# Batches 0 and 1 of an attention on 64x32 tiles, all engines in one written order until unit 32

## The chip, the core and the metric

The kernel runs on one core of one Trainium2 chip. The core has a matrix engine (TensorE, PE in the rows; PEld is its weight load), a vector engine (VectorE, DVE), a scalar engine (ScalarE, ACT), a general engine (GpSimd, POOL) and a queue engine that issues the DMAs (SyncE, SP). The metric is the device time of one launch in microseconds. Three runs of the kernel before took 1621.26 to 1624.84 us, with a median of 1621.86 us.

## The reference

Three layers follow one another: a two-step attention, a feed-forward layer with a leaky rectifier, and a gated feed-forward layer.

```python
# q, k, v: 8 batches, 8 heads, 576 tokens, 64; p: 8, 8, 32, 64
p_packed = sm_attn(p, k, v)                  # softmax(scale * p k^T) v
x = sm_attn(q, p_packed, p_packed)           # to 4608 tokens x 512
h = x @ w_in                                 # 512 x 2048
g = np.maximum(h, 0.0) + alpha * np.minimum(h, 0.0)
x = g @ w_out                                # 2048 x 512
g = x @ w_gate                               # 512 x 1536
out = (g / (1.0 + np.exp(-g)) * (x @ w_val)) @ w_out2
```

## The kernel before

The first feed-forward layer is cut into 256 units: 16 token halves of 288 tokens (batch b, half), times 16 blocks f of 128 hidden columns. A unit has an h part (`h_unit`, six 128x288 matmuls on `a2`, the attention weights, and `ppw`, the product of packed values and `w_in`), then ScalarE, VectorE, ScalarE and GpSimd make the rectified `g32` and its split in a rounded `hi` and a rest `lo`. Three units later its o part (`o_unit`, twelve 128x288 matmuls) adds to four PSUM banks `acc0` to `acc3`. A run of units with one token half ends with the four banks being emptied; where the sum is not complete, it goes to DRAM as `x1p` and is read again by `load_part` and added at the end of that token half's next run. Units are numbered in the order of the list `order`.

`w_in` and `w_out` come as 16 pieces of 1 MB in a 64-bit format (`i0` to `i14`, `o0` to `o14`, two blocks f each) and are widened to 32 bits: two ScalarE, three VectorE (lines 244, 248, 257) and two GpSimd instructions a piece; a `w_out` piece is then rounded (`round_piece`). `ppw` of batch b and four blocks f (`pp_win`, the words `w00`, `w01` and so on) needs two `w_in` pieces and the batch's packed values.

Batches 2 to 7 have their attention in `attention(b)`: its small matmuls work on 64x32 tiles of the PE array, eight heads at a time (`heads8`), its k and q are loaded in 128-byte pieces and turned by VectorE, and its steps are laid between units by the table STEPS. Batches 0 and 1 have theirs in `quad(g)`, four heads at a time on 128x64 tiles, with k and q turned by PE; four quads a to d. Their steps, the loads and the pieces are ordered by LOADS, START, EARLY and ORDER; a scheduler sets the order on each engine within these. The first 64 units are of batches 0 and 1, in runs of eight blocks f; units 64 to 255 are of batches 2 to 7, in runs of sixteen.

While units go on, from slot GROUP0 (half a unit is a slot) the weights of the last layer are widened too (`more_weights2`). The last layer starts after unit 255.

Of the kernel before, what the change touches and what calls it, by code (L numbers as in the profile page):

```python
# [81 lines left out]
GROUP0 = 84  # L82
# [20 lines left out]
def f32(ap):  # L103
    return ap.bitcast(F32)


@with_exitstack
def tile_kernel(
# [105 lines left out]
    raws, vals, borrowed, queue, marks, spots = [], [], [], [], {}, {}  # L214
    fetched, loaded, unsplit = [], [], []
# [9 lines left out]
    def load():  # L225

        src, parts, f = queue.pop(0)
        raw = raws.pop(0)
        fetch(like(raw, src), src)
        loaded.append((raw, parts, f))  # L230

    def fetch(out, in_):

        with tc.issue_after(fetched[-1].ins) if fetched else ExitStack():
            fetched.append(nc.sync.dma_start(out=out, in_=in_))

    def widen(raw, val):
# [3 lines left out]
        nc.scalar.activation(out=f32(val), in_=f32(high), func=AF.Abs)  # L241
        nc.scalar.activation(out=low, in_=low, func=AF.Copy, scale=2.0**-29)
# [22 lines left out]
        yield "v"  # L265
        yield "v"
# [4 lines left out]
    def convert():  # L271

        raw, parts, f = loaded.pop(0)
        dst = parts()
        spots["piece"] = spots.get("piece", -1) + 1
        if f is None:
            val = dst[0].bitcast(U32)
        else:
            val = vals.pop(0) if len(vals) > 1 else vals[0]
        for _ in widen(raw, val):  # L280
            pass
        if queue and (spots["piece"] < 4 or not any(raw is t for t in borrowed)):
            raws.append(raw)
            load()
        unsplit.append((dst, val, f))

    def round_piece():

        dst, val, f = unsplit.pop(0)
        for i in range(2 if f is not None else 0):  # L290
# [6 lines left out]
            nc.gpsimd.tensor_tensor(out=lo, in0=full, in1=f32(hi), op=ALU.subtract)  # L297

# [14 lines left out]
    make_identity(nc, ident)  # L313
    ppbd = [sm.tile([P, P], F32, name=f"ppbd{i}") for i in range(2)]
    for t in ppbd:
        nc.vector.memset(t, 0.0)
    al = sm.tile([P, NF1], F32, name="al")
    sg = sm.tile([P, NF1], F32, name="sg")
    sal = sm.tile([P, NF1], F32, name="sal")
    spare = sm.tile([P, 1], F32, name="spare")  # L320
    a2, ppT = {}, {}

    def quad(g, ptags=("at",), evac=nc.scalar):

# [37 lines left out]
        def s_v():  # L362
            st["v"] = load_n(v, "v")
# [1281 lines left out]
```

## Time and profile before

| | us |
|---|---|
| median of three runs | 1621.86 |
| the profiled execution | 1619.38 |
| its span, first to last instruction | 1617.6 |
| PE busy in the span | 1557.8 |
| VectorE, ScalarE, GpSimd busy | 999.8, 777.7, 986.5 |

The profile is of one execution. Busy time is time in which an engine ran an instruction of the program; "idle before" names what ended an engine's wait. PEclk is the TensorE clock that was granted, as a share of full speed; its mean over the span is 0.989. A tile name such as `h` stands for all buffers of that name.

### The profile page before, as it was taken

To read this page: it belongs to the slowest core of one execution; us is meant where nothing else is said; L and a number is where in the kernel's file an instruction comes from. 1 tells how busy PE (TensorE), PEld (TensorE's weight loads), DVE (VectorE), ACT (ScalarE), POOL (GpSimd) and SP (SyncE) were. 2 spreads that over 40 slices of the span, in tenths; PEclk is the share of its full clock that TensorE was granted. 3 is DMA by queue.
4 is the path that set the end of the run, shared out by engine and by line. 5 is a ranking of instruction groups with operands and counts; after the bars stand their busy time and mean duration, and the time that the engine had idled before them with its cause. 6 is when DMAs were issued, how large, how long until landed. Compare 5 with 4: busy or idle time off the path is not lost.

```text
span 1617.6 us, 30288 instructions
## 1 busy us (share of the span) xinstructions
PE 1557.8 (96%) x10967; PEld 1467.5 (91%) x10967; DVE 999.8 (62%) x1788; ACT 777.7 (48%) x1722; POOL 986.5 (61%) x1057
## 2 busy tenths in 40 slices
PE   6589999999999999999999999999999999999997
PEld 3368898989898989889999999999999999999997
DVE  5856557564646556474346765685686676578556
ACT  6577655666565656565443333333333333333322
POOL 3637655767676665657266566665666656666653
PEclk8799999999999999999999999999999999999999
DMA  9515365756555564653567788688688777866962
GB/s 293 146 43 149 103 167 152 187 146 174 139 166 158 143 178 129 176 172 112 192 228 270 258 280 279 239 295 273 250 301 247 276 277 264 292 240 245 295 251 70
DMA packets 296358, 333.88 MB, mean 206 GB/s; under 512 B 193536, under 2 KB 247824, under 8 KB 291600
## 3 DMA queue, kind: packets, MB, share of 16 engines
q1 hardware_dynamic: 296208, 331.94, 64.2%
q8 instruction: 86, 1.41, 0.4%
q14 instruction: 64, 0.52, 0.1%
HBM read 276.05 MB, written 55.84 MB: 205 GB/s over the span
## 4 chain that ended last, share of the span: by engine, by line
PE 83%; DVE 6%; ACT 4%; issue 2%; DMA 2%; POOL 1%; SPq 1%; ACTq 0%; POOLq 0%; DVEq 0%
PE acc L1099 7%; PE acc L1105 7%; PE acc L1100 7%; PE yb L308 5%; PE yb L310 4%; PE yb L309 4%; PE h L308 4%; PE h L310 3%; PE h L309 3%; PE xb L308 3%; PE vb L309 3%; PE vb L308 3%; PE vb L310 3%; PE xb L309 3%; PE xb L310 3%
## 5 line engine op out<-in xcount | busy, mean ns | idle before, releaser
L1086 POOL TENSOR_TENSOR lo<-g,hi 128x288 fp32r<-128x288 f32 x256 | 219.5, 861 | 208.9 <-ACT hi L1084 150.0
L1076 DVE SCALAR_TENSOR_TENSOR g<-h,sg,m 128x288 f32<-128x288 f32 x256 | 130.7, 512 | 214.9 <-ACT m L1073 179.2
L1309 POOL TENSOR_TENSOR s<-s,u 128x384 f32<-128x384 f32 x72 | 73.0, 1014 | 210.1 <-ACT s L1302 210.1
L1341 POOL TENSOR_TENSOR s<-s,s 128x384 f32<-128x384 f32 x141 | 150.2, 1065 | 48.0 <-DVE s L1306 34.2
L1263 DVE TENSOR_TENSOR u<-yb,p 128x384 f32<-128x384 f32 x144 | 80.0, 556 | 157.5 <-PE yb L310 132.8
L308 PE MATMUL h<-a2h,ppw 128*128 128x288 f32 x512 | 158.9, 310 | 14.2 <-ACT a2h L543 7.1
L1073 ACT ACTIVATE m<-h,sal 128x288 f32<-128x288 f32 x256 | 127.1, 497 | 87.5 <-PE h L310 87.0
L1084 ACT ACTIVATE hi<-g 128x288 fp32r<-128x288 f32 x256 | 112.7, 441 | 93.0 <-DVE g L1076 85.9
L309 PE MATMUL h<-a2h,ppw 128*128 128x288 f32 x512 | 151.8, 297 | 0.0
L310 PE MATMUL h<-a2l,ppw 128*128 128x288 f32 x512 | 151.5, 297 | 0.0
L1335 POOL TENSOR_TENSOR fl_S<-s,fh_S 128x384 fp32r<-128x384 f32 x142 | 147.1, 1045 | 0.2
L308 PE MATMUL yb<-ring,gv 128*128 128x384 f32 x432 | 145.5, 337 | 1.4 <-DVE u L1263 1.4
L310 PE MATMUL yb<-ring,gv 128*128 128x384 f32 x432 | 144.4, 334 | 0.0
L309 PE MATMUL yb<-ring,gv 128*128 128x384 f32 x432 | 144.4, 334 | 0.0
L308 PEld LDWEIGHTS h<-a2h,ppw 128*128 128x128 f32 x512 | 97.1, 190 | 44.0 <-issue 16.2
L1263 DVE TENSOR_TENSOR u<-vb,u 128x384 f32<-128x384 f32 x144 | 80.0, 556 | 81.3 <-PE vb L310 80.9
L1335 POOL TENSOR_TENSOR fl_A<-s,fh_A 128x384 fp32r<-128x384 f32 x108 | 113.3, 1049 | 25.2 <-ACT fh_A L1331 23.9
L1302 ACT ACTIVATE s<-p 128x384 f32<-128x384 f32 x72 | 37.8, 525 | 179.5 <-DVE p L1263 179.5
L1331 ACT ACTIVATE fh_S<-s 128x384 fp32r<-128x384 f32 x144 | 72.7, 518 | 70.2 <-POOL s L1341 67.4
L966 POOL TENSOR_TENSOR cva<-cva,cva 128x256 fp32r<-128x256 f32 x126 | 92.6, 744 | 12.7 <-ACT cva L965 12.2
L308 PE MATMUL xb<-ring,gv 128*128 128x384 f32 x288 | 98.5, 342 | 1.6 <-ACT p L1285 1.4
L309 PEld LDWEIGHTS h<-a2h,ppw 128*128 128x128 f32 x512 | 97.5, 190 | 0.0
(298 smaller groups left out, 4923.9 us busy)
## 6 DMA issues: line engine op xcount, KB each, us to landing
gv<-wgvd SPq DMA_DIRECT2D x144, 896.0 KB, 7.4
wp<-wo2d SPq DMA_DIRECT2D x36, 1024.0 KB, 5.1
wp<-wo2d SPq DMA_DIRECT2D x36, 768.0 KB, 4.5
wgvd<-cva SPq DMA_DIRECT2D x84, 256.0 KB, 2.8
wo2d<-cva SPq DMA_DIRECT2D x42, 256.0 KB, 2.8
v<-in_v_dram SPq DMA_DIRECT2D x16, 576.0 KB, 5.2
cva<-in_moe_w_in_dram SPq DMA_DIRECT2D x7, 1024.0 KB, 7.6
kr<-in_k_dram SPq DMA_DIRECT2D x96, 72.0 KB, 2.8
```

Of the source, the lines that this page charges most:

```text
L308: nc.tensor.matmul(o, wlo, xhi, start=start, stop=False, **kw)
L309: nc.tensor.matmul(o, whi, xhi, start=False, stop=False, **kw)
L310: return nc.tensor.matmul(o, whi, xlo, start=False, stop=stop, **kw)
L1073: begun[it] = marks[f"u{it}"] = nc.scalar.activation(out=m, in_=hp, func=AF.Copy, scale=sal[:, f : f + 1])
L1076: made[it] = marks[f"m{it}"] = nc.vector.scalar_tensor_tensor(out=g32, in0=hp, scalar=sg[:, f : f + 1], in1=m, op0=ALU.mult, op1=ALU.max)
L1086: nc.gpsimd.tensor_tensor(out=lo, in0=x, in1=f32(hi), op=ALU.subtract)
L1099: nc.tensor.matmul(acc[dc], lo[:, f % WP, c], ghi, start=start, stop=False)
L1100: last = nc.tensor.matmul(acc[dc], hi[:, f % WP, c], ghi, start=False, stop=False)
L1105: last = nc.tensor.matmul(acc[dc], hi[:, f % WP, c], glo, start=False, stop=stop)
L1263: ins = nc.vector.tensor_tensor(out=out, in0=bank, in1=x, op=ALU.add)
L1335: return (nc.vector if by_dve else nc.gpsimd).tensor_tensor(out=lo, in0=x, in1=f32(hi), op=ALU.subtract)
L1341: engine.tensor_tensor(out=out, in0=x, in1=y, op=op)
```

## The change

`quad` goes away. All eight batches use `attention(b)`, so the matmuls of batches 0 and 1 work on 64x32 tiles too, with eight heads at once. Batch 0 is special: its k is still turned by PE (`s_turn_pe`), its q comes in groups of four heads (`s_half`), its heads are dealt to the tiles by `head0`, its packed values are kept twice, and its second softmax is done by halves of 288 tokens. Batch 1 loads k and q in 128-byte pieces, as batches 2 to 7 do.

START is now one list of all steps up to unit 31, units included: h and O words are the parts of a unit (each word advances it by one engine's share), C and R widen and round a piece, l loads one, w makes a `ppw` (a and b are its column halves), D stores and X loads a partial sum. `Lane` ties every instruction of these steps to the one before it on its engine, so the engines keep that order. The rest of the pieces (`i12`, `i14`, `o12`, `o14`) is laid into units 32 to 51 by LATER, and GROUP0 goes from 84 to 104.

The order of units is now: batch 0's two halves with blocks 0 to 3, the same with blocks 4 to 7, batch 1's halves with blocks 0 to 7, then all four halves with blocks 8 to 11, and all four with blocks 12 to 15. Until unit 63 there are 14 runs in place of 8.

The rectifier is written differently (`rests`, `h_unit`): ScalarE makes max(-h, 0), and VectorE multiplies that by 1 - alpha and adds h. The signs that were folded into `w_out` go, and with them one ScalarE instruction for each half of a `w_out` piece. `widen` yields "v" three times a piece in place of five, which `more_weights2` counts.

```diff
-LOADS = "a.k pd b.k l al a.v b.v l a.q b.q l l"
+LOAD_PART = 4
...
 START = """
-    a.kt0 b.kt0 a.pt a.kt1 b.kt1 b.pt 1 turn a.s1 a.et a.pp b.s1 1:E0,mx1 sign:mx1 c.k c.q c.v a.ppt b.et
...
+    0.v1 0.k0 lo0 al 0.k1 0.p 0.kt0 0.v0 0.kt0 0.k2 Co0 turn 0.k3 li2 turn 0.kt1 Co0 sign 0.pt 0.kt1
+    0.pt 0.q0 Co0 Co0 0.kt2 Co0 0.kt2 0.kt3 Co0 0.kt3 0.q1 0.s11 Ro0 0.s10 Ci2 Ro0 0.mx0 Ci2 1.p 0.mx1
...
+SCRIPTED = 32
+RAWS = """
+    i0:0 i2:1 o0:2 o2:3 i4:4 i6:0 o4:1 o6:2 i8:0 i10:1 o8:0 o10:1 i12:0 i14:1 o12:0 o14:0
+"""
...
-GROUP0 = 84
+GROUP0 = 104
...
+class Lane:
...
+        def call(*args, **kwargs):
+            if not self.held:
+                return fn(*args, **kwargs)
+            with self.tc.issue_after(self.last.ins) if self.last else ExitStack():
+                self.last = fn(*args, **kwargs)
+            return self.last
...
-        yield "v"
-        yield "v"
         yield "p"
...
             full = like(f32(val), dst[0])[:, i, :]
-            nc.scalar.activation(
-                out=full, in_=full, func=AF.Copy, scale=sg[:, f + i : f + i + 1]
-            )
             nc.scalar.activation(out=hi, in_=full, func=AF.Copy)
...
         with behind():
             for i in range(H // 2):
                 for r in range(2):
-                    rows, n = slice(64 * r, 64 * r + 64), slice(32 * i, 32 * i + 32)
+                    n = slice(32 * i, 32 * i + 32)
                     last = nc.tensor.matmul(
-                        out[r][n], lhs[rows, n], rhs[i][rows], start=True, stop=True
+                        out[r][n], lhs(r, n), rhs(r, i), start=True, stop=True
...
+    def head0(r, i):
+
+        return 4 * r + (i ^ r)
+
+    def lhs_of(b, r, e, n):
+
+        if b == 0:
+            n = slice(P * r + n.start, P * r + n.stop)
+        return ppT[b][rows(e), n]
...
+        def s_half(half):
+
+            t = wide[half][:, : 2 * S]
+            for i in range(2):
+                st["q"][2 * half + i] = t[:, i * S : (i + 1) * S]
+            for r in range(2):
+                h = 4 * r + 2 * half
+                src = q[b, h : h + 2].rearrange("i (t j) (e x) -> e j (i t) x", j=32, x=32)
+                for e in range(2):
+                    blk = 2 * r + e
+                    nc.sync.dma_start(
+                        out=t[32 * blk : 32 * blk + 32].rearrange("p (t x) -> p t x", x=32),
+                        in_=src[e],
+                    )
...
+        def s_turn_pe(i):
...
+                for x in range(M6 // 2):
+                    nc.tensor.transpose(
+                        tp[:, x * PB : (x + 1) * PB],
+                        st["k"][i][:, hh, x * P : (x + 1) * P],
+                        ident[:PB, :PB],
+                    )
...
+            for half in range(2) if first else (None,):
+                c = 14 + 2 * r + half if first else 4 + r
+                nc.scalar.activation(
+                    out=e[:, span(half)],
+                    in_=st["s1"][half][r] if first else e,
+                    func=AF.Exp,
+                    bias=sums[:, 2 + r : 3 + r],
+                    scale=SCALE,
+                    accum_out=sums[:, c : c + 1],
+                )
...
+        def s_rest(r, half=None):
+            hi, lo = (t[:, span(half)] for t in a2[b, r])
+            engine = nc.gpsimd if early else nc.vector
+            engine.tensor_tensor(
+                out=lo, in0=st["a"][r][:, span(half)], in1=f32(hi), op=ALU.subtract
+            )
...
+    def pp_win(b, j, c=slice(0, 512)):
+
+        if (b, j) not in ppw:
+            ppw[b, j] = wtile("C", F32R, f"ppw{b}_{j}")
+        t = ppw[b, j]
...
+        heads8(o, lambda r, n: lhs_of(b, r, at_head(r, n.start // 32)[0], n), rhs)
+        yield
+        for r in range(2):
+            nc.scalar.activation(out=t[:, r, c], in_=o[r], func=AF.Copy)
+        yield
+        for r in range(2):
             nc.vector.tensor_tensor(
-                out=t[:, NQ + q2, :], in0=o, in1=f32(t[:, q2, :]), op=ALU.subtract
+                out=t[:, NQ + r, c], in0=o[r], in1=f32(t[:, r, c]), op=ALU.subtract
...
-    for bs in [(0, 1)] + [(b,) for b in range(2, B)]:
-        for fs in (range(NF1 // 2), range(NF1 // 2, NF1)) if len(bs) > 1 else (range(NF1),):
-            for j in range(2 * bs[0], 2 * bs[-1] + 2):
-                order += [(j, f, f == fs[0], f == fs[-1]) for f in fs]
+    runs = [((0, 1), 0, 4), ((0, 1), 4, 8), ((2, 3), 0, 8)]
+    runs += [((0, 1, 2, 3), 8, 12), ((0, 1, 2, 3), 12, 16)]
+    runs += [((2 * b, 2 * b + 1), 0, NF1) for b in range(2, B)]
+    for js, f0, f1 in runs:
+        for j in js:
+            order += [(j, f, f == f0, f == f1 - 1) for f in range(f0, f1)]
 
...
         spots["slot"] = slot
-        left = dict(v=vector, p=2, s=1, a=1, w=99)
+        left = dict(v=vector, p=2, s=1, a=1, n=99, w=99)
...
+        yield
         g32 = gp.tile([P, HS], F32, tag="g32", name=f"g32_{it}", bufs=2)
         m = gp.tile([P, HS], F32, tag="r", name=f"m_{it}", bufs=2)
-        begun[it] = marks[f"u{it}"] = nc.scalar.activation(
-            out=m, in_=hp, func=AF.Copy, scale=sal[:, f : f + 1]
+        begun[it] = nc.scalar.activation(out=m, in_=hp, func=AF.Relu, scale=-1.0)
+        yield
+        made[it] = nc.vector.scalar_tensor_tensor(
+            out=g32, in0=m, scalar=away[:, f : f + 1], in1=hp, op0=ALU.mult, op1=ALU.add
         )
-        made[it] = marks[f"m{it}"] = nc.vector.scalar_tensor_tensor(
-            out=g32, in0=hp, scalar=sg[:, f : f + 1], in1=m, op0=ALU.mult, op1=ALU.max
-        )
-        gs[it] = split(gp, g32, it, LAG1 + 1, LAG1)
...
+        for i in range(2) if pr is None else (pr,):
+            nc.sync.dma_start(out=dst[:, 2 * i : 2 * i + 2, :], in_=sums1[it][i])
+
+    starts, seen = [it for it in range(N1) if order[it][2]], set()
+    for it in starts:
+        j = order[it][0]
+        if j in seen and it >= SCRIPTED:
+            at(it + LOAD_PART, 0, lambda j=j: load_part(j))
+        seen.add(j)
 
...
 
+    run(START)
+    assert not going
+    written.clear()
     due = []
-    for it in range(N1 + LAG1):
+    for it in range(SCRIPTED, N1 + LAG1):
         if it == CHAIN0:
             chained.append(it)
         steps(it, 0)
         if it < N1:
-            h_unit(it)
+            all_of(h_unit(it))
         steps(it, 1)
-        due.extend(range(max(it - LAG1, 0), it - LAG1 + 1))
```

What this does to the order shows at three places. First VectorE, from the transposes that end the attention ahead of unit 0 (`a`, and `first0`, `first1` in the new kernel) to the first rectified units `g32`. Before:

```order
L542 STREAM_TRANSPOSE a_0_407<-s2t_0_379 128x288
L542 STREAM_TRANSPOSE a_1_417<-s2t_1_392 128x288
L244 TENSOR_SCALAR wi1_452<-wi1_452 128x4x256
L248 TENSOR_SCALAR wi1_452<-wi1_452 128x4x256
L257 SCALAR_TENSOR_TENSOR wi1_452<-cva0_104,wi1_452 128x4x256
L244 TENSOR_SCALAR cvb0_109<-cvb0_109 128x1024
L248 TENSOR_SCALAR cvb0_109<-cvb0_109 128x1024
L257 SCALAR_TENSOR_TENSOR cvb0_109<-cvc0_106,cvb0_109 128x1024
L1076 SCALAR_TENSOR_TENSOR g32_0_512<-h0_505,sg_101,m_0_513 128x288
L1076 SCALAR_TENSOR_TENSOR g32_1_549<-h1_542,sg_101,m_1_550 128x288
```

The same place in the new kernel (`u1` and `u3` are turned k of batch 1, `av` a `w_out` piece, `b4` batch 0's second half of the softmax):

```order
L141 STREAM_TRANSPOSE first0_122<-b3_108 128x288
L141 STREAM_TRANSPOSE first1_123<-b4_109 128x288
L141 TENSOR_TENSOR ppw0_0_426<-ppw0_00_470,ppw0_0_426 128x256
L141 TENSOR_TENSOR ppw0_0_426<-ppw0_01_471,ppw0_0_426 128x256
L141 STREAM_TRANSPOSE u3_116<-u7_120 128x576
L141 STREAM_TRANSPOSE u1_114<-u5_118 128x576
L141 TENSOR_SCALAR av_104<-av_104 128x1024
L141 TENSOR_TENSOR b4_109<-b4_109,sx_0_125 128x288
L141 TENSOR_SCALAR av_104<-av_104 128x1024
L141 SCALAR_TENSOR_TENSOR g32_0_523<-m_0_524,away_99,h0_503 128x288
L141 SCALAR_TENSOR_TENSOR av_104<-cvc1_112,av_104 128x1024
L141 TENSOR_REDUCE sx_0_125<-b4_109 128x9
```

Two whole pieces stood between the attention and unit 0's `g32`; now it is two thirds of a piece and two transposes of batch 1, and the rest follows behind `g32`.

Second PE, at the first units. Before, units 0 and 1 (`h0`, `h1`) stood in turns, first with the heads of quad a (`a2h_0`), then with those of quad b (`a2h_1`):

```order
L308 MATMUL h0_505<-a2h_0_405,ppw0_0_441 128x288
L309 MATMUL h0_505<-a2h_0_405,ppw0_0_441 128x288
L308 MATMUL h1_542<-a2h_0_405,ppw0_0_441 128x288
L309 MATMUL h1_542<-a2h_0_405,ppw0_0_441 128x288
L310 MATMUL h0_505<-a2l_0_406,ppw0_0_441 128x288
```

Now the logits of batch 1 (`s110_1`, `s111_1`, on 64x32 tiles) stand between units 0 and 1:

```order
L141 MATMUL h0_503<-a2h0_0_484,ppw0_0_426 128x288 x2
L141 MATMUL h0_503<-a2l0_0_485,ppw0_0_426 128x288
L141 MATMUL h0_503<-a2h1_0_487,ppw0_0_426 128x288 x2
L141 MATMUL h0_503<-a2l1_0_488,ppw0_0_426 128x288
L141 MATMUL s110_1_512<-u0_113,pT_1_381 32x288
L141 MATMUL s111_1_513<-u0_113,pT_1_381 32x288
L141 MATMUL s110_1_512<-u1_114,pT_1_381 32x288
L141 MATMUL s111_1_513<-u1_114,pT_1_381 32x288
```

Units 0 and 1 no longer stand in turns, and batch 1's logits follow the first unit at once.

Third the DMA queue, at the store of the first partial sum (`x1p0_3`, token half 0 after unit 3) in the new kernel; `kr0_2` to `kr2_2` are k of batch 2, `u5` q of batch 1:

```order
L141 DMA u5_118<-in_q_dram 32x18x32 x4
L139 DMA kr0_2_1787<-in_k_dram 32x18x32 x4
L139 DMA kr1_2_1792<-in_k_dram 32x18x32 x4
L141 DMA x1p0_3_716<-x1s3_0_717 128x576
L139 DMA kr2_2_1813<-in_k_dram 32x18x32
L141 DMA x1p0_3_716<-x1s3_1_754 128x576
```

The store stands behind eight loads of batch 2, and all four loads of `u5` stand ahead of those.

## Rows read from the trace of the kernel before

**Rows 1.** Busy time in five stretches; columns: stretch, length, engines' busy us (instructions), PEclk, DMA.
```profile
0.00:53.80 53.80, 28.06 (x152) 16.78 (x152) 33.88 (x66) 30.58 (x63) 22.04 (x36) 0.82 0.98 272
...
53.80:137.90 84.10, 70.28 (x453) 52.31 (x454) 54.86 (x88) 61.69 (x130) 44.69 (x39) 0.91 0.25 77
...
137.90:177.20 39.30, 39.26 (x286) 37.27 (x285) 21.35 (x35) 29.61 (x55) 29.22 (x29) 1.00 0.49 154
...
177.20:269.90 92.70, 89.81 (x805) 80.46 (x804) 54.11 (x101) 53.45 (x119) 52.05 (x57) 1.00 0.55 145
...
269.90:801.30 531.40, 525.30 (x4699) 487.01 (x4699) 299.36 (x541) 320.03 (x750) 338.20 (x413) 1.00 0.57 160
```

**Rows 2.** The same stretches, instructions on tile h alone (PE, PEld, DVE, ACT).
```profile
53.80:137.90 84.10, 18.91 (x96) 15.31 (x97) 7.99 (x16) 7.93 (x16) 0.91 0.25 77
...
177.20:269.90 92.70, 31.40 (x193) 27.08 (x194) 15.91 (x31) 15.41 (x31) 1.00 0.55 145
```

**Rows 3.** PE in order of time, 0 to 54; columns: start, us, what, idle before.
```profile
6.05 1.19 PE L382 MATMUL kt<-ident,k 96*128 96x96 f32 x6 [6.05 <-DMA k<-in_k_dram]
...
53.83 0.61 PE L308 MATMUL h<-a2h,ppw 128*128 128x288 f32 x1 [6.49 <-ACT a2h L543]
```

**Rows 4.** PE in order of time, at 79.8, 199.6 to 203 and 247.
```profile
79.82 1.90 PE L803 MATMUL ppw<-wi,ppT 128*64 128x512 f32 x8
...
199.65 0.30 PE L308 MATMUL h<-a2h,ppw 128*128 128x288 f32 x1
...
202.06 0.30 PE L308 MATMUL h<-a2h,ppw 128*128 128x288 f32 x1
...
202.94 0.71 PE L572 MATMUL s<-kT,pT 64*32 64x288 f32 x16
...
247.13 1.09 PE L572 MATMUL ppw<-wi,ppT_2b 64*32 64x512 f32 x16
```

**Rows 5.** VectorE's forms, 0 to 180; columns: form xcount, busy us, mean ns, idle before.
```profile
L1076 DVE SCALAR_TENSOR_TENSOR g<-h,sg,m 128x288 f32<-128x288 f32 x34 | 17.1, 509 | 21.7 <-ACT m L1073 15.7 <-POOL lo L1086 5.9
...
L257 DVE SCALAR_TENSOR_TENSOR wi<-cva,wi 128x1024 uint32<-128x1024 uint32 x7 | 10.7, 1523 | 0.1
...
L808 DVE TENSOR_TENSOR ppw<-ppw,ppw 128x512 fp32r<-128x512 f32 x12 | 8.1, 680 | 1.2 <-ACT ppw L807 1.2
...
L248 DVE TENSOR_SCALAR wi<-wi 128x1024 uint32<-128x1024 uint32 x8 | 7.2, 901 | 0.1
...
L244 DVE TENSOR_SCALAR wi<-wi 128x1024 f32<-128x1024 f32 x8 | 5.5, 686 | 2.6 <-ACT wi L241 2.6
...
L510 DVE TENSOR_TENSOR s2t<-s2t,sx 128x288 f32<-128x288 f32 x4 | 3.8, 955 | 0.1
...
L422 DVE TENSOR_REDUCE mx<-s 128x1 f32<-128x288 f32 x8 | 3.5, 454 | 8.1 <-PE s L409 8.0
...
L542 DVE STREAM_TRANSPOSE a<-s2t 128x576 f32<-128x576 f32 x2 | 1.4, 752 | 0.0
```

**Rows 6.** Line 257, 0 to 180; columns: form xcount, ns min/median/max, first and last start.
```profile
L257 DVE SCALAR_TENSOR_TENSOR cvb<-cvc,cvb x2: 1226/1696/2167, 61.8 to 78.1; 128x1024 uint32<-128x1024 uint32 x2
```

**Rows 7.** ScalarE's forms, 0 to 180.
```profile
L430 ACT ACTIVATE E<-s,mx 128x288 f32<-128x288 f32 x8 | 3.9, 491 | 4.3 <-DVE mx L426 4.3
```

**Rows 8.** Busy time, PEclk, DMA share and GB/s in three short stretches.
```profile
5.00:10.00 5.00, 3.15 (x16) 2.59 (x17) 0.22 (x1) 2.58 (x7) 2.74 (x12) 1.00 1.07 295
...
45.00:50.00 5.00, 0.81 (x4) 0.45 (x3) 5.00 (x11) 0.00 (x0) 3.03 (x3) 0.52 1.08 259
...
202.00:204.00 2.00, 2.00 (x27) 1.37 (x26) 0.29 (x1) 1.04 (x3) 0.80 (x1) 1.00 0.79 130
```

**Rows 9.** The DMA queue's issues in order of time, at 200.
```profile
200.10 4.09 SPq L605 DMA_DIRECT2D qr<-in_q_dram  x8
```

**Rows 10.** DMA issues by line: xcount, KB each, median us to landing.
```profile
x1p<-x1s SPq DMA_DIRECT2D x8, 288.0 KB, 2.1
...
x1p<-x1p SPq DMA_DIRECT2D x8, 288.0 KB, 3.2
```

More of the change, by code (lines that the diff above doesn't have):

```diff
@@ L223, in halves_of, with load @@
         return [ap[:, i * n // 2 : (i + 1) * n // 2] for i in range(2)]
[L225 to L235, printed above, removed]
+    def load(name):
+        src, _, _ = jobs[name[0], int(name[1:])]
+        nc.sync.dma_start(out=like(raw_of[name], src), in_=src)
     def widen(raw, val):
@@ new lines, in alloc, with span, blocks, pair_of @@
+        def alloc(name):
+            return homes[b][name] if early else utile("u", [P, S], f"{name}_{b}")
+        def span(half):
+            return slice(0, S) if half is None else slice(half * HS, (half + 1) * HS)
+        def blocks(half):
+            return slice(0, NB32) if half is None else slice(half * NB32 // 2, (half + 1) * NB32 // 2)
+        def pair_of(src, i):
+            if not first:
+                return src[b, 2 * i : 2 * i + 2]
+            h0, h1 = (head0(r, i) for r in range(2))
+            return src[b, h0 : h1 + 1 : h1 - h0]
@@ L759, in s_rest, with t3 @@
[L759 to L761 removed]
+            s2 = logits(
+                lambda r, n: lhs_of(b, r, r, n),
+                lambda r, i: st["qT"][i ^ r if first else i],
+                half,
+                "s2",
+            )
+            yield
+            for r in range(2):
+                nc.vector.transpose(out=st["s2"][r][:, span(half)], in_=s2[r])
+        def t3(r, half):
+            return st["s2"][r][:, span(half)].rearrange("p (t j) -> p t j", j=NP)
@@ new lines, in s_sum, with s_rs, s_mul @@
+        def s_sum(r, half=None):
+            nc.vector.tensor_reduce(out=small(r, half), in_=t3(r, half), axis=AX.X, op=ALU.add)
+            if r and not early:
+                s_rs()
+        def s_rs(half=None):
+            t = sx[:, :, blocks(half)]
+            nc.vector.tensor_scalar_add(t, t, 1e-9)
+            nc.vector.reciprocal(out=t, in_=t)
+        def s_mul(r, half=None):
+            t = t3(r, half)
+            nc.vector.tensor_tensor(out=t, in0=t, in1=spread(r, half), op=ALU.mult)
@@ new lines, in pp_win, with at_head, rhs @@
+        o = [
+            ps.tile([P, 512], F32, tag="at", name=f"ppw{b}_{j}{r}", bufs=2)[:, c] for r in range(2)
+        ]
+        def at_head(r, i):
+            h = head0(r, i) if b == 0 else 2 * i + r
+            return h % 2, h // 2
+        def rhs(r, i):
+            e, chunk = at_head(r, i)
+            return w[rows(e), chunk, c]
+        heads8(o, lambda r, n: lhs_of(b, r, at_head(r, n.start // 32)[0], n), rhs)
+        yield
+        for r in range(2):
+            nc.scalar.activation(out=t[:, r, c], in_=o[r], func=AF.Copy)
@@ L838, in run, with all_of @@
+    for r in range(2):
+        for home in homes:
+            home[f"E{r}"], home[f"s2t{r}"] = thirds[r], wide[r][:, 2 * S : 3 * S]
+        homes[0][f"a{r}"] = atile(f"first{r}", F32)
+        homes[1][f"a{r}"] = thirds[r]
+    twice = homes[0]["a0"][:, : 2 * P]
+    groups = {str(b): attention(b) for b in range(2)}
+    def all_of(parts):
+        for _ in parts:
+            pass
+    going = {}
     def run(script):
         for word in script.split():
-            word, _, held = word.partition(":")
```

736 lines of the change are left out of this document (313 added, 423 removed).

## The prediction

> **What bounds the kernel now.** I read the stages first, then the units in them, then the waits. The stages [rows 1] are cut at units 0, 16, 32 and 64: the matmuls on tile `h` [rows 2] are 96 from 53.8 to 137.9, so 16 units of six, and 193 from 177.2 to 269.9, so 32 but for a stray one. From 269.9 on PE is busy 525.3 of 531.4 us: nothing the change does early can speed up what follows, it can only let it begin sooner. A unit costs PE 2.41 us when nothing else is due, from one `h` to the next [rows 4] (199.65 to 202.06). So the 32 units up to 177.2 need 77 us, and the stretch from 53.8 took 123.4; another 53.8 went before unit 0. These 177 us are what can shrink. The wait at unit 0 is the clearest: PE sat idle for 6.49 us until ScalarE's `a2h` [rows 3], while VectorE, which feeds it, was busy for all of 45 to 50 [rows 8]. After that PE worked 70.3 of 84.1 us [rows 1], a good part of it on attention and `ppw`, and at a granted clock of 0.91.
>
> **How I work it out.** The new kernel keeps the unit's matmuls, so I need four times: unit 0, unit 17 (about where VectorE stops being the one that ends last), unit 32, unit 64. Counts are from the new order; durations from the rows.
>
> **Unit 0.** K of batch 0 must land first. Before, the first 0.59 MB had landed at 6.05 [rows 3], and loads then ran at 0.295 MB/us [rows 8]. The new queue puts v (0.59), `o0` (1.05), k (1.18), v (0.59) and 0.07 of small loads until the last k: 3.48 MB, so 6.05 + 2.89/0.295 = 15.8. `i2` follows at 19.4. Then q, 1.18 MB in 128-byte pieces: such loads ran at 130 GB/s with a share of 0.79 [rows 8], 165 at full share, so 7.2 us and 26.6. From the last k on: transposes 0.7, four copies at about 0.45, two halves of logits at 0.71 [rows 4], the maximum (two at 0.454 [rows 5] and two small ones), four exponentials at 0.49 [rows 7] and their sums, four E copies and `pp`, `ppt`. I put 14 us on this chain (the matmuls and copies on it add up to 12.4, and 1.6 for handing over, both estimates from these rows), so the second logits come at 30; q is there in time. From their first result to the transposes that end the attention VectorE has 27 instructions: one piece 3.1 (0.686 + 0.901 + 1.523), five broadcasts at 0.955, thirteen light ones of 288 columns at 0.45, two of 576 at 0.752, two half `ppw` at 0.34, two small: 16.7. That is 46.7, and unit 0 starts near 47.5 instead of 53.8. Bounds: 45 without hand-over, 53 if the 128-byte loads take twice as long.
>
> **Units 0 to 17.** From there to unit 17's `g32` VectorE has 91 instructions in its written order: 18 `g32` at 0.509 = 9.2; seven pieces at 3.1 = 21.8; 14 of 576 columns at 0.752 = 10.5; four broadcasts of 576, between 0.955 and twice that, taken at 1.2 = 4.8; three of 288 at 0.955 = 2.9; six `ppw` at 0.68 and two halves = 4.8; 15 light ones at 0.45 = 6.8; eight small at 0.25 = 2.0. Sum 62.8, all durations from [rows 5]. PE's own work from unit 0 to 17 is 46 (18 h parts at 0.8, 15 o parts at 1.6, batch 1's attention and three `ppw`), so VectorE ends last. ScalarE and GpSimd have fewer and no longer instructions there than VectorE. I add 4 us for waits at the head of VectorE's queue (an estimate; between none, as from 45 to 50 [rows 8], and the 21, explained below, of its share before): 67. Unit 17's `g32` is done at 46.7 + 67 = 113.7. PE may run at its lower clock level, 1.2 GHz, for some of the first units, as it did in 45 to 50 with a granted clock of 0.52 [rows 8], after having had little to do; with VectorE last I count that at nothing, and at 3 us if PE becomes last.
>
> **Units 17 to 32.** `h17` is computed 1.5 us before its `g32`. From there PE has 15 h parts (12.0), 14 o parts (22.4) and two `ppw` at 1.02 to 1.09 [rows 4] (2.0): 36.4. VectorE has 33 instructions in it, some 20 us, so PE ends last. Unit 32 starts at 113.7 - 1.5 + 36.4 = 148.6, against 177.2.
>
> **Units 32 to 64.** Before: 92.7, PE busy in 89.8 [rows 1]. Both kernels do batch 2's attention there. Two `ppw` of batch 1 go from 1.90 for eight records [rows 4] and the waits between them (6 us for the pair with idle PE, an estimate from this and the 2.9 idle) to two at 1.0: -4.0. Four more run ends, each with four VectorE additions of about 0.45, and three more pieces lie here: VectorE was busy 54 of 92.7 [rows 1] and gets some 17 more, so it stays under PE; I put 3 us on what it delays, between 0 and 10. So 91.7, and unit 64 starts at 240.3 against 269.9: 29.6 earlier.
>
> **After unit 64.** The last layer's weights are widened later (GROUP0) and closer together; in the order they end at unit 222 instead of 239. PE lacked 6.1 us in 531 [rows 1]; I add 1, between 0 and 3. The ScalarE instructions that go with the signs (16) and the new form of `m` and `g32` (same shapes) lie beside PE: nothing, and if `m` were dearer by 0.05 in 256 units, still nothing, as ScalarE is busy 320 of 531.
>
> **Sum.** 29.6 - 1 = 28.6 off the profiled execution's 1619.4 (span 1617.6 and 1.8 around it): 1590.8. The median of the runs is 2.5 above the profiled one: 1593.
>
> **A rule of the skill.** The same VectorE instruction took from 1226 to 2167 ns [rows 6], the long ones beside GpSimd's work. The Trainium skill, GPSIMD Engine Reference, section Specifications, says that GpSimd's way into SBUF is shared with VectorE, with contention for instructions with two SBUF inputs or in a two-port mode; the trace agrees with 2167 against 1226, and its means hold both kinds. By the rule a denser stretch makes these instructions longer; that is the second rival.
>
> **Rivals.**
> 1. VectorE keeps ahead. Without waits (-4), with every piece at the price of the shortest (2.6 instead of 3.1, seven of them: -3.5), unit 0 at 45 (-2.5), no cost of run ends or later (-4): 14 less, 1579. For it: the order is written out on all engines, so waits could be few. Against: a fixed order cannot dodge a late landing.
> 2. VectorE and GpSimd get in each other's way. With shared instructions at 1.77 times the shortest (2167/1226), a piece takes 4.6, seven cost 10.5 more, seven broadcasts 2.5: +13, 1606. For it: GpSimd was busy 44.7 of 84 [rows 1] and now does the same splits in less time. Against: the means hold much of it already.
> 3. Waits in VectorE's queue. It was busy 54.9 of 84.1 [rows 1], a share of 0.65. At 0.75 the 62.8 become 84, 17 more than my 67: 1610; at 0.65 they are 97 and the gain is nothing.
> 4. Slower: partial sums that come late. Store 2.1, load 3.2 [rows 10] and four issues at 0.51 [rows 9] make 7.3 us from one run end to the next use, and runs now end every four units, 9.6 us. Where 16 loads of k or q stand ahead in the queue (8.2 us, [rows 9]), the addition waits for some 6 us, VectorE behind it, then PE for its banks. Ten of the new run ends need such a load, against four. The gain is used up at the fifth such wait; with seven of them it costs 42, so 1635. Against: PE lacks only 2.9 us over four such run ends before [rows 1].
>
> **How the numbers follow.** My forecast 0.56 (1586 to 1601), rival 1 0.14, rival 2 0.12, rival 3 0.11, rival 4 0.07. The range for 8 in 10 goes from 1578 to 1611: it leaves out the best of rival 1, the worst of rival 3, and rival 4. 0.2% is 3 us, about what can be told from no change. Faster by more: all but rival 4 and the end of rival 3, 0.91; within it 0.03; slower 0.06.
>
> **What would show it.** Right: the first `h` at 45 to 50, the 192 matmuls of `h` to unit 32 ended by 145 to 153, the next 192 in 89 to 94 more, VectorE busy over 90% from 30 to 114, and the rest unchanged within 3 us. Wrong: VectorE under 80% there with PE waiting behind it (rival 3); the median of line 257's like above 1.7 us (rival 2); PE waiting for the banks after the run ends at units 35, 39, 43 (rival 4).

## The result, and the profile after

The changed kernel took 1600.71 us (median of four runs, 1598.94 to 1609.37), the kernel before beside it 1621.94 us. The ratio is 0.9876, with a 95% interval of 0.9839 to 0.9914. The forecast was 1593, inside a range of 1578 to 1611: about 21 us were gained where 28.6 were expected (18.0 by the two profiled executions, 19.2 in the control run below). The profiled execution of the changed kernel has a span of 1599.6 us, at a mean granted clock of 0.99.

| start of | before | changed | forecast |
|---|---|---|---|
| unit 0 | 53.8 | 43.6 | 47.5 |
| unit 17 | | 107.9 | 112.2 |
| unit 32 | 177.2 | 147.8 | 148.6 |
| unit 64 | 269.9 | 242.2 | 240.3 |
| the last layer | 801.3 | 781.5 | 772.7 |
| end of the span | 1617.6 | 1599.6 | 1589.0 |

The forecast's row for the last layer puts the whole 1 us for later weights ahead of it.

The start of a unit does not stand for the same work in both kernels. PE's matmuls on `acc` up to the first `h` of unit 64 (columns: stretch, length, busy us of PE, PEld, VectorE, ScalarE with counts, PEclk, DMA), before and changed:

```profile
0.00:269.86 269.86, 109.64 (x732) 100.82 (x732) 8.10 (x20) 2.92 (x8) 0.94 0.53 150
```

```profile
0.00:242.15 242.15, 107.61 (x720) 99.86 (x720) 15.86 (x40) 3.23 (x8) 0.94 0.66 178
```

That is 61 o parts of twelve matmuls before and 60 now, at the same 384 matmuls on `h`; at unit 32 it is 30 and 29. One o part, 1.6 us of PE, has moved behind these marks and is paid later.

The stages of the changed kernel, cut at its units 0, 16, 32 and 64 and at the first matmul of the last layer (columns as in [rows 1]):

```profile
0.00:43.60 43.60, 19.85 (x233) 9.84 (x234) 27.40 (x59) 22.97 (x46) 10.99 (x15) 0.82 0.91 215
43.60:105.50 61.90, 53.16 (x486) 43.28 (x487) 53.50 (x84) 40.87 (x83) 46.42 (x38) 0.91 0.77 201
105.50:147.80 42.30, 40.60 (x311) 37.38 (x310) 25.74 (x39) 22.27 (x46) 27.72 (x26) 1.00 0.38 130
147.80:242.20 94.40, 91.25 (x821) 82.03 (x820) 58.76 (x112) 49.95 (x112) 48.02 (x49) 0.98 0.61 168
242.20:781.50 539.30, 531.38 (x4712) 491.47 (x4712) 297.52 (x551) 304.49 (x761) 353.00 (x427) 1.00 0.59 166
```

VectorE, the third pair, went from 54.9 of 84.1 us [rows 1] to 53.5 of 61.9: it has the largest share in the first sixteen units now, as forecast; whether it ends last there is tested below. From 242.2 on, though, 539.3 us pass where 531.4 passed before. 1.6 us of that are the o part; why some 6 more were given back later is the question.

VectorE's two stretches of the forecast, from the second logits to the end of the attention and from there to unit 17's `g32`:

```profile
30.40:43.10 12.70, 4.99 (x48) 1.23 (x48) 12.01 (x28) 6.97 (x12) 2.52 (x2) 0.50 0.82 164
43.10:108.90 65.80, 56.56 (x511) 46.70 (x512) 57.40 (x90) 41.78 (x85) 48.24 (x39) 0.91 0.74 195
```

Of the 8.4 idle us in the second, 6.27 are one wait. Four engines in order of time, PE, VectorE, ScalarE and the DMA queue, show where it comes from (start, duration, instruction, and in brackets the idle time before it and what ended it):

```profile
89.38 0.69 PE L141 MATMUL acc<-lo,wo1h 128*128 128x288 f32 x4
95.52 0.85 PE L141 MATMUL h<-a2h,ppw 128*128 128x288 f32 x2 [5.45 <-DVE g L141]
```

```profile
86.86 0.50 DVE L141 SCALAR_TENSOR_TENSOR g<-m,away,h 128x288 f32<-128x288 f32 x1
93.63 1.41 DVE L141 TENSOR_REDUCE sx<-b 128x18 f32<-128x576 f32 x2 [6.27 <-ACT b L141]
```

```profile
84.38 0.45 ACT L141 ACTIVATE hi<-g 128x288 fp32r<-128x288 f32 x1 [1.45 <-DVE g L141]
91.39 1.12 ACT L141 ACTIVATE wi<-cva 128x1024 f32<-128x1024 f32 x1 [6.57 <-DMA cva<-in_moe_w_in_dram]
92.41 0.62 ACT L141 ACTIVATE wo1h<-b 128x512 fp32r<-128x512 f32 x1
92.93 1.25 ACT L141 ACTIVATE b<-b 128x576 f32<-128x576 f32 x2
```

```profile
69.76 5.42 SPq L139 DMA_DIRECT2D kr<-in_k_dram  x8
...
78.72 0.65 SPq L141 DMA_DIRECT2D cva<-in_moe_w_in_dram  x1
79.41 5.17 SPq L139 DMA_DIRECT2D kr<-in_k_dram  x5
84.75 1.05 SPq L141 DMA_DIRECT2D cva<-in_moe_w_in_dram  x1
```

Read from the bottom: sixteen 128-byte loads of batch 2's k (`kr`, first turned at 161.7) were issued from 69.8 on, the piece `i10` behind them at 84.75. It landed at 91.4. ScalarE stood at the head of its written order for it, with the exponentials of batch 1's second softmax (`b`) behind; VectorE stood for those, with units' `g` behind; PE stood for `g`. Then PE ran at its lower level, 1.2 GHz: the granted clock of the next four us was 0.54. After a wait of 2.15 us at 155 it was 0.55.

```profile
95.50:99.50 4.00, 3.98 (x17) 3.98 (x18) 3.71 (x8) 4.00 (x8) 0.90 (x2) 0.54 0.00 2
...
157.40:161.00 3.60, 3.60 (x16) 3.60 (x17) 2.21 (x5) 1.72 (x5) 1.57 (x2) 0.55 0.44 159
```

After unit 64 it is ScalarE again. These are its waits from there to the last layer (total us, times, longest), in the kernel before and in the changed kernel; `cva` holds the last layer's weights while they are widened:

```profile
ACT cva L965 <- POOL cva L269: 11.7, 16, 1.1
...
ACT cva L965 <- POOL cva L983: 6.7, 12, 1.0
```

```profile
ACT cva L139 <- POOL cva L139: 45.1, 52, 2.8
```

18.4 us of standing behind GpSimd (19.1 with a third line of 0.7) became 45.1. All that is queued behind it on ScalarE then waits too: the units' `m`, for which VectorE's `g` and then PE wait, and the steps of the attention. How it reaches PE shows less clearly. PE stands idle for 7.9 us of this stretch in the changed kernel, against 6.1 before; 6.5 us of it are for ScalarE's attention steps (5.5 before), and only 0.2 for `g`:

```profile
PE ppt L139 <- ACT ppbd L139: 2.1, 3, 1.0
PE pp L139 <- ACT ET L139: 1.6, 2, 0.9
PE s L139 <- ACT E L139: 1.5, 2, 1.2
...
PE h L139 <- DVE g L139: 0.2, 1, 0.2
```

Where the rest of the lost time stands in PE's rows is not shown: PE counts as busy 531.4 us in place of 525.3, and the o part is only 1.6 of these 6.1. The cause is therefore tested by runs.

### The profile page after: what moved, and what is told of

Read it like the earlier page. It is cut to its first block, busy times and chain, and to the rows that moved or that the text cites. A ratio compares the mean times of both kernels' runs of the same rounds, so it can differ in the third digit from the quotient of the medians.

```text
span 1599.6 us, 30662 instructions
## 1 busy us (share of the span) xinstructions
PE 1544.1 (97%) x11132; PEld 1460.7 (91%) x11132; DVE 1000.4 (63%) x1803; ACT 722.8 (45%) x1652; POOL 987.5 (62%) x1037
## 4 chain that ended last, share of the span: by engine, by line
PE 81%; DVE 5%; issue 4%; POOL 3%; DMA 3%; ACT 2%; SPq 1%; POOLq 0%; ACTq 0%; DVEq 0%
PE acc L139 18%; PE yb L139 14%; PE vb L139 9%; PE h L139 9%; PE xb L139 9%; PE o_at L139 6%; PE o_h L139 6%; PE o_acc L139 4%; POOL cva L139 2%; PE ppw L139 2%; PE acc L141 1%; PE s L139 1%; DVE ring L139 1%; POOL lo L139 1%; DMA cva<-in_moe_w_val_dram 1%
## 5 line engine op out<-in xcount | busy, mean ns | idle before, releaser
L139 PE MATMUL yb<-ring,gv 128*128 128x384 f32 x1296 | 260.8, 335 | 1.3 <-DVE u L139 1.3
L139 DVE SCALAR_TENSOR_TENSOR g<-m,away,h 128x288 f32<-128x288 f32 x224 | 114.1, 510 | 200.8 <-ACT m L139 157.4
L139 PEld LDWEIGHTS yb<-ring,gv 128*128 128x128 f32 x1296 | 227.4, 188 | 4.1 <-DVE u L139 4.1
L139 PE MATMUL h<-a2h,ppw 128*128 128x288 f32 x896 | 192.0, 303 | 2.3 <-DVE g L139 2.3
L139 PE MATMUL vb<-ring,gv 128*128 128x384 f32 x864 | 173.7, 335 | 0.0
L139 PEld LDWEIGHTS xb<-ring,gv 128*128 128x128 f32 x864 | 151.8, 188 | 5.6 <-ACT p L139 2.9
L139 PEld LDWEIGHTS vb<-ring,gv 128*128 128x128 f32 x864 | 153.2, 188 | 0.0
L139 ACT ACTIVATE hi<-g 128x288 fp32r<-128x288 f32 x224 | 98.6, 440 | 91.4 <-DVE g L139 86.0
L139 ACT ACTIVATE cva<-cva 128x256 fp32r<-128x256 f32 (+4 forms) x204 | 102.7, 525 | 80.9 <-POOL cva L139 45.8
L139 POOL TENSOR_TENSOR cva<-cva 128x256 f32<-128x256 f32 (+1 forms) x108 | 103.6, 959 | 37.7 <-DVE cva L139 13.1
L139 ACT ACTIVATE m<-h 128x288 f32<-128x288 f32 x224 | 90.2, 404 | 65.0 <-PE h L139 64.4
```

The lines of the kernel that those rows point to most:

```text
L139: return fn(*args, **kwargs)
```

## Experiments

Times are medians; ratios are to the kernel before, run beside each group (1620.44, 1622.46 and 1622.30 us).

**The late landing.** Batch 2's k loads are held back behind the load of a partial sum:

```diff
+    def behind_part(step):
+        with tc.issue_after(spots["part"].ins):
+            all_of(step() or ())
...
+                if b == 2 and n in ("k0", "k1", "k2", "k3"):
+                    at(*divmod(slot, 2), lambda step=steps_of[n]: behind_part(step))
+                    continue
...
+        if written:
+            spots["part"] = nc.sync.last
```

> The changed kernel with one edit: the sixteen 128-byte loads of batch 2's k may not be issued before the partial sums of the second runs have been fetched (about 115 us instead of 70 us). My theory: in the changed kernel ScalarE stood 6.57 us at 84.8 until i10 had landed at 91.4, because i10's load was issued behind these sixteen; VectorE stood 6.27 us behind ScalarE, PE 5.45 us behind VectorE, and PE then ran at a granted clock of 0.81 from 90 to 108. If so, unit 32 starts at 139 to 143 instead of 147.8 and the time falls by 5 to 9 us, to 1592 to 1596. Rival: VectorE was busy 55.9 of 64.3 us from unit 0 to 17 and would end nearly as late without the wait: at most 2 us, 1599 to 1601. Second rival: the loads come late for batch 2's own attention in units 36 to 40 and the gain is lost there: unit 64 at 240 or later.

Measured: 1594.54 us, ratio 0.9838 (0.9823 to 0.9853). The loads went out from 98.7 us on, `i10` is no longer waited for, and VectorE is busy 95% from unit 0 to 17:

```profile
44.10:103.80 59.70, 54.96 (x504) 44.43 (x505) 56.69 (x88) 41.44 (x85) 47.83 (x39) 0.94 0.71 199
...
142.60:235.40 92.80, 89.74 (x820) 80.52 (x820) 59.16 (x112) 49.88 (x112) 47.22 (x49) 1.00 0.62 171
```

Unit 32 starts at 142.6, unit 64 at 235.4. The theory held, at 6 to 9 us (the changed kernel was 1600.7 and, below, 1603.2), and neither rival did.

**What the weights of the last layer cost.** First the two edits on them alone, in the kernel before:

```diff
-GROUP0 = 84
+GROUP0 = 104
...
-        yield "v"
-        yield "v"
         yield "p"
```

> The kernel before with only the two edits on the last layer's weights: GROUP0 104 in place of 84, and widen yields v three times a piece in place of five. The changed kernel was 27.7 us ahead at unit 64 and 19.9 us ahead at the first matmul of the last layer. Theory: the later and denser weight work takes these 7.8 us, because its ScalarE instructions stand ahead of the attention's: then this kernel loses 4 to 8 us, 1626 to 1630, nearly all of it between units 64 and 112. Rival: the loss has another cause (it lies between units 64 and 112, where the o parts of units 61 to 63 are also paid): then within 2 us of 1622.

Measured: 1627.56 us, 1.0043 (1.0029 to 1.0057): 7.1 slower. Unit 64 stayed at 270.0, and from there to the last layer it took 540.6 us, against 531.5. The theory held on the amount, not on the place: the loss was spread, 4.5 us of it between units 208 and 224, where the mean granted clock was 0.97 (1.00 elsewhere behind unit 64). Here PE did wait for `g`, 5.2 us in all. Then one `yield "v"` put back, in the changed kernel:

> The changed kernel with one more v in widen, four a piece in place of three, so that the last layer's weights are spread over more units; five a piece do not end before the last layer begins. Same question from the other side. Theory that the denser weights cost the time after unit 64: 2 to 4 us faster, 1597 to 1599. Rival, another cause: within 1 us of 1600.7.

Measured: 1604.84 us, 0.9903 (0.9888 to 0.9918). That is not faster, and speaks against spreading as the remedy. The changed kernel itself was run beside the next three, as a control:

> The changed kernel as it is, beside the other runs of this call, because the same instructions up to unit 32 took 147.8 us in one profile and 151.1 in another (the run with four v). Expected: 1598 to 1605, with the profile's unit 0 at 43 to 46 and unit 32 at 147 to 152. If it comes out at 1604 or more, the run with four v is no slower than the changed kernel, and says nothing against the theory that the weight work is to blame.

Measured: 1603.22 us, 0.9890 (0.9873 to 0.9906), unit 0 at 44.2, unit 32 at 148.6. So a fourth `v` neither helps nor harms by much. From unit 64 to the last layer the two took 541.4 and 541.0 us. The third one on this was the kernel before with the two `yield` lines gone, GROUP0 left at 84:

> The kernel before with one of the two edits on the last layer's weights: widen yields v three times a piece in place of five, GROUP0 stays at 84. Both edits together cost 7.1 us (1627.6 against 1620.4). Theory: the density does it, since a piece's instructions then come in two slots in place of three and stand ahead of the units' own: 1624 to 1629. Rival: the later start does it: within 2 us of 1620.4, and PE's waits on g and x1s after unit 64, 7.3 us in the run with both edits, are not there.

Measured: 1631.97 us, 1.0061 (1.0048 to 1.0074): 9.5 slower. The density costs; the later start doesn't. It may save some, since work that begins at slot 84 also lies beside units 42 to 64: units 32 to 64 took 94.7 us, against 92.7 (at a granted clock of 0.98, against 1.00). (Unit 64 came 3.6 us later, but 1.6 of that was there at unit 32, ahead of any of this work.) From unit 64 to the last layer it took 539.2 us. PE's waits for `g` and `x1s` there were 6.1 us, and ScalarE's for GpSimd had gone up:

```profile
ACT cva L963 <- POOL cva L267: 22.6, 27, 2.6
ACT cva L963 <- POOL cva L981: 18.3, 23, 2.0
```

So I changed the theory: not the number of instructions in a slot, but the distance between GpSimd's step on a piece and ScalarE's rounding of it. Two runs on the kernel with k held back test that. The first has `SETTLE = 3` in place of 2:

> The run with batch 2's k loads held back, with SETTLE 3 in place of 2: ScalarE's rounding of a widened piece of the last layer stands one slot (half a unit) later behind GpSimd's additions. From unit 64 to the last layer the kernel before took 531.5 us, with v three times a piece 539.2, and there ScalarE stood 40.9 us at the head of its queue for GpSimd's work on these pieces, against 18.4 before. Theory: that standing is what holds ScalarE's m, then g, then PE; with the slot between, the stretch takes 532 to 536 in place of 539.0, and the time is 1588 to 1592. Rival: the weights still come in fewer units than before and the engines lack the time whatever the distance: 538 to 541, within 1.5 us of 1594.5.

Measured: 1589.40 us, 0.9804 (0.9787 to 0.9822), 535.1 us from unit 64 to the last layer, in place of 539.0. The second adds:

```diff
-            if kinds[0] == "s" and left["p"] < 2:
+            if kinds[0] == "s" and slot < spots.get("less", 0) + 2:
                 return
+            if kinds[0] == "p":
+                spots["less"] = slot
```

> The run with SETTLE 3, and also one slot more between GpSimd's subtractions on the last layer's weights and ScalarE's rounding of what they give. ScalarE stood 18.3 us for those with v three times a piece, 6.7 us before. Theory: 1 to 3 us less again, 1586 to 1590, and the stretch from unit 64 to the last layer 531 to 534. Rival: the work ends later and collides with the load of the last layer's first weights: no better than with SETTLE 3 alone.

Measured: 1585.43 us, 0.9779 (0.9762 to 0.9795), and 529.8 us for that stretch. ScalarE's wait in it, and all that is left of PE's:

```profile
ACT cva L139 <- POOL cva L139: 11.2, 15, 2.0
```

```profile
PE h L139 <- DVE g L139: 0.7, 2, 0.3
PE pp L139 <- ACT ET L139: 0.3, 1, 0.3
PE s L139 <- ACT E L139: 0.2, 1, 0.2
```

The wait for GpSimd was 41.0 us with k held back alone, 41.9 with four `v`, 32.4 with SETTLE 3 and 11.2 here; PE's idle time in the stretch was 8.5, 9.9, 4.3 and 1.2, and the time followed. For the first step it did not follow the spread: with four `v` the weights' stores ran over 476 us (237.9 to 714.4) and nothing was gained, with SETTLE 3 over 472 (231.9 to 704.2) and 5 us were; with k held back alone it was 463. The second step is less clean. Its stores run over 505 us (230.3 to 735.8), so that its 4 us can come from the distance, from the spread or from both; no run tells these apart. This version beats both kernels, the changed one by 15 to 18 us.

**What carries the first 148 us.** The list START without the ties between instructions:

```diff
-    nc = Lanes(tc, written)
+    nc = Lanes(tc, [])
```

> The changed kernel with the same list START, but the instructions are not tied to each other on their engines, so that the scheduler may move them. It tells whether the held order is what carries the first 148 us. Theory: the order in which the pieces stand around the attention of batches 0 and 1 is the gain, and the scheduler departs from it: unit 0 later than 47, unit 32 at 152 to 165, time 1605 to 1618. Rival: the work on 64x32 tiles and the order of units are the gain and the ties add nothing: unit 32 within 3 us of 147.8, time 1598 to 1604.

Measured: 1627.23 us, 1.0043 (1.0028 to 1.0058): slower than the kernel before. Unit 0 started at 73.9, after PE had waited 8.27 us:

```profile
73.86 0.61 PE L139 MATMUL h<-a2h,ppw 128*128 128x288 f32 x1 [8.27 <-ACT a2h L139]
```

From unit 0 on the loss got no larger: unit 32 came at 176.4. The ties are worth 24 to 27 us here, more than all that the change gains. Ahead of 73.9 VectorE was busy 56.7 us, against 27.4 ahead of unit 0 with the ties: the scheduler filled the attention's way with other work. This went further than my theory had it (1605 to 1618, unit 32 at 152 to 165). It shows that the rest of the change gains nothing without the ties, not that the ties alone would do: the 64x32 tiles, the order of units and a held order in the kernel before were not run apart.

**Does VectorE end last, and what does GpSimd do to it?** With k held back, GpSimd's addition of the low words left out in the written order:

```diff
-        for a, b in zip(halves_of(val), halves_of(low)):
+        for a, b in zip(halves_of(val), halves_of(low)) if not written else ():
```

> The run with batch 2's k loads held back, in which GpSimd leaves out the addition of the low words in the pieces of the written order, so those weights lose their low words. GpSimd loses two instructions of about 1.3 us a piece in 13 pieces. It asks two things at once: does VectorE end last from unit 0 to 17, and how much do GpSimd's instructions lengthen VectorE's? In the changed kernel the seven pieces of that stretch took VectorE 24.8 us, against 18.1 at the price of the shortest instructions. Theory: both hold, the pieces fall to 18 to 20 us, and unit 17 comes 5 to 8 us earlier than at 103.8. Rival: PE, busy 55.0 of 59.7 us there, ends last as soon as VectorE gets faster: unit 17 at most 3 us earlier.

Measured: 1588.79 us, 0.9794 (0.9781 to 0.9807), unit 17 at 98.1 in place of 103.8. Of the 5.7 us 1.1 were won ahead of unit 0; from unit 0 to 17 it took 55.1 us in place of 59.7:

```profile
43.00:98.10 55.10, 52.56 (x503) 44.57 (x504) 51.73 (x86) 40.96 (x84) 30.67 (x28) 0.94 0.76 217
```

VectorE was busy 5.0 us less and the stretch got 4.6 shorter, with VectorE's share still at 94%: it ends last there rather than PE, the rival. That GpSimd, with 17 us less to do there, gave a part of this by itself is not excluded. The seven pieces took VectorE 21.5 us in place of 24.7: less than half of what I had put down to GpSimd's additions as too long went with them. GpSimd's other work (`lo`) still lies beside. VectorE's rows for one `w_out` piece from unit 0 to 17, in the changed kernel and in this one (form xcount, busy us, mean ns, idle before):

```profile
L141 DVE SCALAR_TENSOR_TENSOR cvb<-cva,cvb 128x1024 uint32<-128x1024 uint32 x1 | 1.7, 1704 | 0.0
...
L141 DVE TENSOR_SCALAR cvb<-cvb 128x1024 f32<-128x1024 f32 x1 | 1.7, 1660 | 0.0
...
L141 DVE TENSOR_SCALAR cvb<-cvb 128x1024 uint32<-128x1024 uint32 x1 | 0.9, 881 | 0.0
```

```profile
L141 DVE SCALAR_TENSOR_TENSOR cvb<-cva,cvb 128x1024 uint32<-128x1024 uint32 x1 | 1.2, 1224 | 0.0
...
L141 DVE TENSOR_SCALAR cvb<-cvb 128x1024 f32<-128x1024 f32 x1 | 0.7, 694 | 0.4 <-ACT cvb L141 0.4
...
L141 DVE TENSOR_SCALAR cvb<-cvb 128x1024 uint32<-128x1024 uint32 x1 | 0.7, 685 | 0.0
```

**Two smaller ones.** With k held back, the first two steps of `i14` moved from slots (34, 0) and (34, 1) to (36, 1) and (37, 0):

> The run with batch 2's k loads held back, and with one more edit: the first two steps of widening i14 are moved from units 34 and 34.5 to units 36.5 and 37. In the changed kernel ScalarE stood 1.68 us at 152.6 for i14 to land, VectorE 3.32 us behind it, and PE 2.1 us for g at 155, after which the granted clock was 0.89 for the stretch from 147.8 to 160. Theory: unit 64 starts 2 to 4 us earlier than in the run with k held back alone (235.4), and the time is 1591 to 1593. Rival: i14 is then late for the ppw of unit 51, and the wait comes back there: within 1 us of 1594.5.

Measured: 1594.56 us, 0.9828 (0.9815 to 0.9842), unit 36 at 152.5 in place of 153.0, unit 64 at 235.2 in place of 235.4. The rival held as to the time: nothing. And the new rectifier alone in the kernel before:

```diff
...
-            out=m, in_=hp, func=AF.Copy, scale=sal[:, f : f + 1]
+            out=m, in_=hp, func=AF.Relu, scale=-1.0
...
-            out=g32, in0=hp, scalar=sg[:, f : f + 1], in1=m, op0=ALU.mult, op1=ALU.max
+            out=g32, in0=m, scalar=sal[:, f : f + 1], in1=hp, op0=ALU.mult, op1=ALU.add
```

> The kernel before with the new rectifier alone: ScalarE makes max(-h, 0), VectorE multiplies by 1 - alpha and adds h, and the signs and the 16 ScalarE instructions that folded them into w_out are gone. The prediction counted this at nothing, since it lies beside PE. Expected: within 2 us of 1621.5, g32 still at 0.50 to 0.52 us and m at 0.39 to 0.42. Rival: ScalarE, busy 61.7 of 84.1 us from unit 0 to 16, ends last there with VectorE behind it, and its 16 instructions of 0.4 to 0.6 us were worth 3 to 8 us: 1613 to 1618.

Measured: 1620.07 us, 0.9987 (0.9977 to 0.9998): 2.2 faster than the kernel before beside it. That is inside the 1619.5 to 1623.5 that I expected, and far from the rival. `m` went from 497 to 406 ns. Unit 16 came at 132.5 in place of 137.9, unit 64 at 268.0 in place of 269.9: most of what was won early was gone again by unit 64. From there to the last layer it took 528.9 us in place of 531.5, and the last layer 818.9 in place of 816.3.

## Why the prediction was right, step by step

The measured time lies inside the range, 7.7 us above the forecast, and the mechanism ahead of unit 64 was right in the main. Some luck is in the number: the span missed by 10.6 us (1599.6 against 1589.0). The forecast put the profiled execution 2.5 us under the median, and this one lay 0.6 over it.

**Unit 0** came 3.9 us earlier than forecast. The loads were priced right: the last k was turned from 14.70 on (forecast 15.8), the second logits began at 29.05 (30). Too high was VectorE's 16.7 from there; it took 12.7. The five broadcasts, priced at 0.955 from [rows 5], took 0.45 each; and VectorE's durations overlap, which a sum of them doesn't see:

```profile
46.40 0.68 DVE L141 TENSOR_SCALAR av<-av 128x1024 uint32<-128x1024 uint32 x1
47.00 0.51 DVE L141 SCALAR_TENSOR_TENSOR g<-m,away,h 128x288 f32<-128x288 f32 x1
47.42 1.22 DVE L141 SCALAR_TENSOR_TENSOR av<-cvc,av 128x1024 uint32<-128x1024 uint32 x1
```

Each starts about 0.08 us before the one ahead ends by its duration.

**Units 0 to 17** took 64.3 us; the forecast had 64.7, with VectorE last. That is right by luck: two errors cancel. The durations add up to 63.4 (forecast 62.8), but VectorE was busy only 57.4, for that overlap; and it waited 8.4, where I had put 4. The share of 57.4 in 65.8 is 87%, and 88% in the stretch of the sign (69.4 of 78.5 us from 30.4 on), less than the 90% that I named. Without the one late landing it is 95% from unit 0 to 17.

**Units 17 to 32** took 39.9, not 36.4. The counts were right (15 h parts, 14 o parts, two `ppw`), but, counted from each start to the next, the o parts took 24.0 in place of 22.4, the `ppw` 3.3 in place of 2.0 and the h parts 12.7 in place of 12.0: PE stood 1.7 us for `g` and for a piece, which this way of counting adds to the part ahead of the wait.

**Units 32 to 64** took 94.4, not 91.7. The saving on batch 1's `ppw` came: one cost 1.26 and the other 1.02, against 6.05 for the pair. The run ends were harmless, and VectorE was busy 4.7 us more than before, not 17. What I had not seen are PE's wait of 2.15 us at 155, for a `g` behind `i14`, and the 3.6 us at the lower clock behind it. With k held back a wait of 2.1 us stayed, the mean granted clock was 1.00 in place of 0.98, and the stretch took 92.8.

**After unit 64** is the step that failed. I put +1, between 0 and 3, and "the rest unchanged within 3 us" was one of my signs; it was 7.8 up to the last layer (539.3 against 531.5). Two things failed. The first is a miscount: my 15 and 14 o parts to unit 32 are 29, where the kernel before has done 30, so a lead at unit 64 still has 1.6 us to pay, and I carried it over whole. The second is the cost of the weights, which in the kernel before alone was 9.1 (540.6 against 531.5; 7.1 by the medians) with both edits and 7.7 with the density alone. I had counted only that the weights come later and closer together on engines with time to spare. The spare time was there, but in queues: an instruction that stands for GpSimd holds all behind it on ScalarE. The rectifier, which I had put at nothing, gave back 2.6 in this stretch of the kernel before, and 2.2 in all. As an estimate, each term from one profile, 1.6 + 9.1 - 2.6 make 8.1, for the 7.8. 1.8 us more are in the last layer itself (818.1 against 816.3); why, stays open.

**The rivals.** Rival 1 had unit 0 at 45 (it was 43.6) and no cost later, which was wrong. Rival 2's mechanism is there, and up to 5.7 us hang on it in the run without the low words, but most of it was in my prices already: the pieces took 24.8, against 21.8 of the forecast and 4.6 each, 32, of the rival. Its sign, a median above 1.7 us for the instruction of line 257, did not come: of the seven from unit 0 to 17 the median was 1.28. The instructions lengthened include one with a single input (1660 ns in the changed kernel, 694 without GpSimd's additions). By the rule of the Trainium skill, GPSIMD Engine Reference, section Specifications, contention is for two SBUF inputs or a two-port mode; the trace agrees if that single-input instruction runs in such a mode, which no row here shows. Rival 3's wait in VectorE's queue happened once, by a late landing, the case named against rival 1; at 87% it stayed far from the 75% at which it would have decided. Rival 4's mark, PE waiting for banks after run ends, did not show: PE's matmuls stood 0.3 us for `x1p` up to unit 32, and not at all from 32 to 64.

## What to carry to other kernels

Where two orders are compared at a mark such as the start of a unit, count what each has done by then: here one o part, 1.6 us, lay on the other side. An order that is held on all engines needs its loads held too: sixteen early loads that nobody waited for cost 6 to 9 us through three queues. For background work on shared engines look at the distance from each producer to its consumer on another engine, not at the share of busy time; a half unit more of it was worth 5 us, and a second one, which also spread the work, 4. When durations are added up for an engine, compare the sum of a stretch with its busy time first.

## What the runs showed of the hardware that I had not expected

The same instructions in the same order, up to unit 32, took 147.8, 148.6 and 151.1 us in three profiles (the changed kernel, the control and the one with four `v`), while their last layers repeat within 1 us. The start is where these differ: unit 0 came at 43.6, 44.2 and 45.4, unit 16 at 105.5, 106.3 and 108.8, and from there to unit 32 it was 42.3 us in all three. And a wait of 2.15 us on PE at 155 was followed by 3.6 us at a granted clock of 0.55; a wait of 2.07 us at 150 with k held back was not, the four us behind it had 1.00. What made the difference stays open.
